# One quarter more of a dense layer's block in seven products: tiles 8 to 11 of block 1, and what moves with them

## The chip, the cores and the metric

The kernel runs on one core of a Trainium2 chip. The core has a matrix engine (TensorE, PE in the profile; its weight loads are the row PEld), a vector engine (DVE), an activation engine (ACT), a general engine (POOL) and a queue engine (SP), each with its own instruction stream; they meet through semaphores. Data moves between the chip's memory and the on-chip buffers by DMAs, which SP, ACT and POOL issue. The time is the device time of one execution in microseconds (us), and less is better. One time of the kernel before is the median of three runs; one further execution was profiled.

## The reference

The input x has 2048 rows of 1024 numbers. The rows are normalised, and the result is the sum of x, a state space branch A and a dense branch B:

```python
xn = _layernorm(x, axis=-1)
return x + _A_ref(xn, ...) + _B_ref(xn, B_w1, B_b1, B_w2)

# A: Lam_bar = exp(dt * Lam), complex
Bu = jnp.einsum("bld,pd->blp", x + 0j, B_bar)
for t in range(L):
    h = Lam_bar[None, :] * h + Bu[:, t, :]
y = 2.0 * jnp.einsum("blp,dp->bld", hseq, Cmat).real + x * Dskip[None, None, :]

# B: 1024 -> 3584 -> 1024
h = jnp.einsum("bsd,df->bsf", x, w1) + b1
sp = jnp.log1p(jnp.exp(-jnp.abs(h))) + jnp.where(h > 0, h, jnp.zeros_like(h))
act = h * jnp.tanh(sp)          # Mish
return jnp.einsum("bsf,fd->bsd", act, w2)
```

## The kernel before

The 2048 rows are worked in four blocks of 512 (`blk` 0 to 3). A block has these stages on PE: dense 1 (x by w1, 28 tiles of 128 columns), the input projection of branch A (x by B, complex), dense 2 (the activations by w2) and the output projection (the scanned state by C). DVE rotates the projected state, scans it over the 512 rows and rotates it back (`rotate_in`, `recur`); at the block's end it adds the two branches to x (`finish`, L1711).

**Plain tiles and quads.** In block 0 all of dense 1 is plain: for each tile, 8 matmuls of 128 x 512 (`first_tile`, L871). From block 1 on parts of it go in seven products: four tiles of w1 (a quad) and the block's 512 rows are split two by two, and seven products of halves stand for eight (`w_product`, L1024). One product is 8 matmuls of 128 x 256. Products 1, 2 and 4 take quarters of the scaled quad; 5, 6, 7 and 3 take sums and differences of quarters, and 5, 6, 7 and 4 sums of x (`sums_x`, L1840). A product lands in one of a quad's three PSUM banks (X, Y, Z; `F_BANKS`); 6, 7 and 4 add to what 1 left in X, and 3 to what 5 left in Z, so that `w_evacuate` must have read a bank before the next product adds to it. There are seven quads of w1, and in the order strings of the diff the letters p q s w x y z name them (`REAL` gives the place of each in w1): p is tiles 12 to 15, q 16 to 19, s 20 to 23, w 24 to 27, x, y and z are tiles 0 to 3, 4 to 7 and 8 to 11. The projection of branch A is done in the same way, for four pairs of column groups, a to d (`product`, L948; `evacuate`). In block 1 (`FAST`) before, tiles 0 to 11 are plain and p, q, s, w are quads; in blocks 2 and 3 (`SPLIT`) all seven are.

**A quad's way.** `w_load` (POOL, four DMAs) brings a quad to an on-chip place (`W_RAW`); `w_scale` (ACT, two instructions) scales it by a power of two; `w_keep` stores quarters 1, 2 and 4 to a scratch in memory (`wsd`); `w_sums` forms 5, 7, 6 and 3 in place (DVE, L1199) and stores them. PE reads quarters back through the ring, seven slots of 512 KB that SP fills in a fixed order of items (`ring_load`); an item's load waits until the slot's user seven items earlier is done. Quads in `ON_CHIP` read products 5, 6, 3 and 7 from the on-chip place.

**Order.** Nothing is scheduled at run time. The strings `WHOLE` (block 1), `STEPS` (block 2) and `LAST` (block 3) are written by hand and read from the left by `project_fast`: a letter and a number are one step (`a5`: product 5 of pair a; `z5`: product 5 of quad z), with its instructions on all engines. Others are `k0` (the next waiting sum on DVE), `P` (`sums_B`, L1833), `T` (`table_scale` on ACT), `V` (`w_scale` of quad s), `v` (of quad w), `h` (`d2_row`, a scaled row group of w2), `j` (`ln_skip`), `r` (`rotate_in`), `g` (Mish on a group of tiles), `u` (`open_unit`: six matmuls of dense 2 in one bank), `l` (the next block's x), `m`, `n` (loads), `Q` (`row_powers`), `S` (`row_scales`), `O` (a held DMA on SP). Each engine then works its own instructions strictly in this order. A DMA of ACT or SP stands in the same stream as its other instructions, and a wait holds up what follows.

**Around block 1.** At block 0's end DVE scales the B matrix and finishes the block (L1820, L1711); then, in `side(0)` of block 1, it forms sums for the projection (L1833), the sums of x (L1840), the sums of quads p and q (L1199) and scales the rest of B (L1820). ACT scales quads, issues block 0's four stores to the output (L1692) and then does the Mish of the plain tiles (L879). The sums of x are written where block 0's rows lay, so they wait for those stores. In block 1's scan, `w_exponent`, `row_powers` and `row_bound` work out scales that blocks 2 and 3 need.

## Time and profile before

| | us |
|---|---|
| median of three runs (lowest, highest) | 587.51 (587.39, 587.77) |
| the profiled execution's own time | 587.58 |
| its span, first to last instruction | 586.3 |
| PE busy in the span | 581.0 |
| DVE busy | 513.4 |
| ACT busy | 401.8 |
| POOL busy | 150.7 |

The span is 1.3 us shorter than the execution's own time; what lies around it is not in the trace. In a timeline a row gives the start (from the span's start), the length, the engine, the line, the operation with its tiles, the number of instructions merged in the row, and in brackets how long the engine had been idle before it and what ended that. Instructions of one engine overlap by up to 0.1 us, so several in a row take less than their number times one. A few per cent of the matmul records are missing, so a count in a row can be lower than the program's. Line numbers are those of the kernel before.

### The profile page before, as it was taken

Reading aid. Unit: us, or ns where it says so; the run is one execution under the profiler, and the core shown is the slowest. Engines: PE = TensorE matmul, PEld = TensorE weight load, DVE = VectorE, ACT = ScalarE, POOL = GpSimd, SP = SyncE. Lnnn points to the kernel's source line nnn. Section 1 sums busy time; section 2 is a strip of 40 time slices with the busy share of each in tenths; the row PEclk is TensorE's granted clock in tenths of the full one; section 3 lists DMA queues with packets and bytes.
Section 4 is the critical chain, followed back from the end, with each engine's and each line's share of the span. In section 5 each row is a group of like instructions: output and inputs, shape, how many; then the busy total and the mean of one; then the engine's idle time right before and its main releaser. Section 6 shows DMA issues by size and latency. Waiting matters only on the chain.

```text
span 586.3 us, 9768 instructions
## 1 busy us (share of the span) xinstructions
PE 581.0 (99%) x3599; PEld 353.9 (60%) x3635; DVE 513.4 (88%) x789; ACT 401.8 (69%) x541; POOL 150.7 (26%) x213
## 2 busy tenths in 40 slices
PE   9999999999999999999999999999999999999998
PEld 8644444444447887444448888644446888844444
DVE  6998999998997878999877889779999669789995
ACT  4859994658578868999916687959223798992330
POOL 2899300123524420441351241001010113100000
PEclk9999999999999999999999999999999999999999
DMA  9999998999688978999999899798865966998832
GB/s 244 306 243 247 245 186 202 316 301 360 185 303 287 357 249 293 316 321 255 345 375 345 305 309 382 257 344 209 306 210 191 346 237 241 326 324 318 293 113 73
DMA packets 116345, 162.15 MB, mean 277 GB/s; under 512 B 55882, under 2 KB 66762, under 8 KB 116298
## 3 DMA queue, kind: packets, MB, share of 16 engines
q1 hardware_dynamic: 99776, 109.67, 62.0%
q0 software_dynamic: 13440, 44.57, 21.7%
q10 hardware_dynamic: 3082, 7.29, 3.3%
q8 instruction: 29, 0.48, 0.3%
q14 instruction: 18, 0.15, 0.1%
HBM read 115.36 MB, written 34.08 MB: 255 GB/s over the span
## 4 chain that ended last, share of the span: by engine, by line
PE 93%; DVE 2%; ACT 2%; DMA 1%; issue 1%; POOL 0%; ACTq 0%; POOLq 0%
PE ps L1502 34%; PE ps L1024 19%; PE ps L948 13%; PE ps L1563 10%; PE ps L871 10%; PE ps L1438 5%; DMA act<-in_A_B_im_dram 1%; PE ps L680 1%; PE ps L689 1%; PE ps L642 1%; ACT act L894 1%; PE ps L1525 1%; ACT act L901 1%; DVE CT L835 0%; DVE CT L833 0%
## 5 line engine op out<-in xcount | busy, mean ns | idle before, releaser
L1502 PE MATMUL ps<-ring,act 128*128 128x512 bf16 x532 | 117.3, 379 | 0.6
L1502 PEld LDWEIGHTS ps<-ring,act 128*128 128x128 bf16 x544 | 53.2, 98 | 63.8
L1044 ACT ACTIVATE snaps<-ps,par,cs 128x256 f32<-128x256 f32 x100 | 54.4, 562 | 44.4 <-PE ps L1024 40.0
L1502 PE MATMUL ps<-ring,hT 128*128 128x512 bf16 x355 | 78.3, 379 | 0.4
L1024 PE MATMUL ps<-TT,ring 128*128 128x256 f16 x552 | 68.3, 273 | 0.0
L910 DVE TENSOR_TENSOR mt<-hT,tab 128x2048 bf16<-128x2048 bf16 (+1 forms) x56 | 67.9, 1213 | 0.4
L1502 PEld LDWEIGHTS ps<-ring,hT 128*128 128x128 bf16 x362 | 35.4, 98 | 42.7
L1453 DVE TENSOR_TENSOR_SCAN hT<-cs,qi,hT 128x512 bf16<-128x512 f32 x48 | 60.7, 1275 | 0.0
L1024 PEld LDWEIGHTS ps<-TT,ring 128*128 128x128 f16 (+1 forms) x552 | 53.8, 98 | 7.2 <-issue 0.2
L871 PE MATMUL ps<-xnT,ring 128*128 128x512 bf16 x258 | 56.8, 379 | 0.3
L1024 PE MATMUL ps<-xnT,ring 128*128 128x256 bf16 x424 | 53.9, 273 | 0.0
L1061 DVE SCALAR_TENSOR_TENSOR act<-ps,cs,snaps 128x512 bf16<-128x512 f32 x54 | 39.8, 748 | 15.2 <-PE ps L1024 13.3
L1024 PEld LDWEIGHTS ps<-xnT,ring 128*128 128x128 bf16 (+1 forms) x424 | 41.4, 98 | 5.4
L871 PEld LDWEIGHTS ps<-xnT,ring 128*128 128x128 bf16 x264 | 25.8, 98 | 30.9
L1230 POOL DMA_DIRECT2D w2d<-act x21 | 15.0, 718 | 110.5 <-ACT act L1240 54.9
L1473 ACT ACTIVATE hT<-hT,wz 128x1024 bf16<-128x1024 bf16 x16 | 18.1, 1146 | 34.3 <-DVE hT L1468 34.3
L1563 PE MATMUL ps<-ring,act 128*128 128x512 bf16 (+1 forms) x176 | 39.5, 379 | 0.2
L1230 POOL DMA_DIRECT2D w2d<-hb x28 | 20.0, 717 | 74.4 <-ACT hb L1240 33.0
L894 ACT ACTIVATE act<-act 128x2048 bf16<-128x2048 bf16 (+3 forms) x13 | 33.0, 2557 | 3.8 <-DVE act L1047 3.8
L973 DVE TENSOR_TENSOR hT<-ps,snaps 128x512 f16<-128x512 f32 x36 | 23.8, 687 | 12.3 <-ACT snaps L965 11.1
L1563 PEld LDWEIGHTS ps<-ring,act 128*128 128x128 bf16 (+1 forms) x180 | 17.6, 98 | 20.6
L1173 POOL DMA_DIRECT2D wsd<-hb x35 | 19.1, 548 | 39.0 <-DVE hb L1199 28.8
(240 smaller groups left out, 1085.2 us busy)
## 6 DMA issues: line engine op xcount, KB each, us to landing
ring<-wsd SPq DMA_DIRECT2D x122, 256.0 KB, 4.6
ring<-in_B_w_dram SPq DMA_DIRECT2D x54, 512.0 KB, 5.9
ring<-ctd SPq DMA_DIRECT2D x24, 512.0 KB, 4.4
ring<-w2d SPq DMA_DIRECT2D x24, 512.0 KB, 4.6
wsd<-hb POOLq DMA_DIRECT2D x35, 256.0 KB, 5.1
ring<-w2d SPq DMA_DIRECT2D x29, 256.0 KB, 3.8
w2d<-hb POOLq DMA_DIRECT2D x28, 256.0 KB, 5.5
w2d<-act POOLq DMA_DIRECT2D x21, 256.0 KB, 6.2
```

Source lines behind the costliest of these rows:

```text
L871: PE.mm(lambda e, k=k, w=w: e.matmul(ps[:, bank, :], lhsT=w, rhs=xnT[:, k, :], start=k == 0, stop=k == NK - 1), reads=[b_ring[s]] + b_xnT, ...
L894: aop(lambda e: e.activation(t, t, AF.Mish), reads=b, writes=b)
L910: vop(lambda e: e.tensor_tensor(mt[:], u.unsqueeze(1).to_broadcast([P, 2, 2, TB]), tab[:, :, j, :].unsqueeze(2).to_broadcast([P, 2, 2, TB] ...
L948: PE.mm(lambda e, w=w, x=x, o=o, begin=begin, end=end: e.matmul(ps[:, bank, o:o + TH], lhsT=w, rhs=x, start=opens and begin, stop=end, ski ...
L1024: PE.mm(lambda e, w=w, x=x, o=o, begin=begin, end=end: e.matmul(ps[:, bank, o:o + TH], lhsT=w, rhs=x, start=opens and begin, stop=end, ski ...
L1044: aop(lambda e, o=o, p=p, j=j: e.activation(o, p, AF.Identity, scale=ig, bias=b1(f0 + j)), reads=[b_ps[b], b_par, b_ig], writes=b_dst)
L1061: vop(lambda e: e.scalar_tensor_tensor(out=dst, in0=bank(b), scalar=ig, in1=src, op0=ALU.mult, op1=ALU.add), reads=[b_ps[b], b_snap[k], b_ ...
L1230: PO.dma(lambda e: e.dma_start(w2d[at // 4][:, at % 4 * TB:(at % 4 + 2) * TB].rearrange("p (j t) -> p j t", j=2), t[:, :, d, :]), sem, rea ...
L1438: PE.mm(lambda e, j=j, ci=ci, k=k, bank=bank: e.matmul(ps[:, bank + ci, :], lhsT=BT[:, ci, j, k, :], rhs=xnT[:, k, :], start=k == 0, stop= ...
L1453: vop(lambda e: e.tensor_tensor_scan(out=hT[:, ci, j, :], data0=cj("r", j).to_broadcast([P, TB]), data1=hT[:, ci, j, :], initial=init, op0 ...
L1502: PE.mm(lambda e: e.matmul(ps[:, u, :], lhsT=lhsT, rhs=rhs, start=st_, stop=last, skip_group_check=blk in SPLIT), reads=reads, writes=[b_p ...
L1563: PE.mm(lambda e: e.matmul(ps[:, bank, :], lhsT=lhsT, rhs=rhs, start=st_, stop=end, skip_group_check=True), reads=b_t + [b_ring[s]], write ...
```

## The change

Quad z (tiles 8 to 11) of block 1 leaves the plain tiles and becomes seven products. Its load and its scaling are done at block 0's end, its sums in block 1 behind those of quad q, and its sums' stores go on POOL; before, it was loaded and scaled in block 1's scan, its sums were formed at block 2's start, and SP stored them there. Products 5, 6, 3 and 7 of z read the on-chip place, which is now act 8 to 15. The order of block 1's products is written anew. `row_powers` for the late rows goes behind the last step of the scan, `row_bound` from the scan to block 2's start (step `S1`), and four sums for w2 go between the four `finish` steps of block 1 instead of ahead of them.

```diff
-    GROUPS = (... (20, 24), (24, 28))
-    TILES = [*range(12)]
+    GROUPS = (... (20, 24), (24, 28), (8, 12))
+    TILES = [*range(8)]
...
-    EARLY, LATE = ((0, 18), (26, 28)), ((18, 26),)
+    EARLY, LATE = ((0, NF),), ((18, 26),)
...
-    WHOLE = ("a2 a1 V0 b2 b1 a5 b5 V1 P4 P5 a6 b6 v6 P6 P7 a3 b3 P0 a7 b7 P1 Q0 n0 p1 q1 a4 b4 "
+    WHOLE = ("a2 a1 V0 b2 b1 a5 b5 V1 a6 b6 a3 b3 k0 k0 a7 b7 k0 k0 P4 P5 z1 q1 a4 b4 z5 P6 P7 v0 z2 q2 P0 P1 q5 z6 P2 q6 z3 P3 q3 T0 "
...
-    STEPS = ("p1 p5 p2 k0 k0 q1 k0 q5 p6 k0 q2 s1 k0 p7 ...
+    STEPS = ("p1 p5 p2 S1 q1 q5 p6 q2 s1 k0 p7 ...
...
-    F_BANKS = ((3, 1, 2), (7, 5, 6), (7, 5, 6), (3, 1, 2))
+    F_BANKS = {0: (3, 1, 2), 1: (7, 5, 6), 2: (7, 5, 6), 3: (1, 2, 3), 6: (3, 1, 2)}
...
-    ON_CHIP = [(5, n) for n in (5, 6, 3, 7)]
+    ON_CHIP = [(i, n) for i in (2, 5) for n in (5, 6, 3, 7)]
...
-    W_RAW = (("h", 0), ("h", 8), ("a", 0), ("h", 8), ("h", 0), ("a", 20), ("h", 8))
+    W_RAW = (("h", 0), ("h", 8), ("a", 8), ("h", 8), ("h", 0), ("a", 20), ("h", 8))
...
-                if i == 2:
-                    held.append(lambda queue: w_store(i, n, o, b_o, queue))
-                else:
-                    w_store(i, n, o, b_o)
+                w_store(i, n, o, b_o)
...
-                row_scales()
+                (row_scales, row_bound)[n]()
...
             elif kind == "v":
-                w_scale(n)
-                w_sums(n, True)
+                w_scale(6, (1 - n,))
+                if n:
+                    w_sums(6, True)
...
             finish(q, 0, len(units) * TB)
+            if blk == FAST:
+                later.pop(0)()
...
                     w_sums(3)
-                    w_load(6)
                     scale_B(2)
                     w_sums(4)
+                    w_load(6)
+                    w_sums(2, True)
                     scale_B(3)
-                if f in (1, 3, 4, 5):
-                    table_scale((1, 3, 4, 5).index(f))
...
                     next(out_stage)
-                    w_load(2)
                     for i in range(2):
                         w_abs(i)
-                    w_scale(2)
                     next(out_stage)
                 if j == 5:
                     w_exponent(1)
-                    row_powers(LATE)
-                    row_bound()
...
+                if j == NJ - 1:
+                    row_powers(LATE)
                     d2_scale(3)
...
         if blk == FAST:
-            for _ in range(4):
-                later.pop(0)()
-            for i in (2, 0, 1):
+            for i in range(2):
                 w_sums(i, True)
...
             w_load(4)
+            w_load(2)
...
             w_load(5)
             w_scale(3)
+            w_scale(2)
```

In block 0's last stage, on POOL: the loads of quads p and q into hb, four small products and the carry of the scan, then the load of quad s into act. Before:

```order
L1098 DMA hb<-in_B_w_dram 128x4x256 x8
L1995 TENSOR_TENSOR cs<-cs 128x8 x2
L1482 TENSOR_TENSOR qi<-hT,cs 128x8 x2
L1482 TENSOR_TENSOR qt<-hT,cs 128x8 x2
L1484 TENSOR_TENSOR qi<-qi,qt 128x8
L1486 TENSOR_TENSOR qi<-qi,qt 128x8
L1098 DMA act<-in_B_w_dram 128x4x256 x4
L1173 DMA wsd<-hb 128x1024 x10
```

and now:

```order
L1099 DMA hb<-in_B_w_dram 128x4x256 x8
L1099 DMA act<-in_B_w_dram 128x4x256 x4
L1994 TENSOR_TENSOR cs<-cs 128x8 x2
L1483 TENSOR_TENSOR qi<-hT,cs 128x8 x2
L1483 TENSOR_TENSOR qt<-hT,cs 128x8 x2
L1485 TENSOR_TENSOR qi<-qi,qt 128x8
L1487 TENSOR_TENSOR qi<-qi,qt 128x8
L1099 DMA act<-in_B_w_dram 128x4x256 x4
L1175 DMA wsd<-hb 128x1024 x3
L1175 DMA wsd<-act 128x1024 x3
L1175 DMA wsd<-hb 128x1024 x11
```

The load of z (four DMAs into act) stands ahead of the four products, and its three quarters' stores between those of p and q.

In block 1, on DVE: the last scaling of B (BT), the joins of the products of pairs a and b with what was kept of them (hT16_49 from PSUM and snaps), the sums of a quad (act) and the sums for the projection (SS_53, BT16_50). Before:

```order
L1820 TENSOR_TENSOR BT<-BT,act 128x2048 x2
L973 TENSOR_TENSOR hT16_49<-ps,snaps_54 128x2x256 x2
L1833 TENSOR_TENSOR SS_53<-BT 128x2x512
L1833 TENSOR_TENSOR SS_53<-SS_53,BT 128x2x512
L1833 TENSOR_TENSOR SS_53<-BT,SS_53 128x2x512
L1833 TENSOR_TENSOR BT16_50<-BT 128x2x512
L973 TENSOR_TENSOR hT16_49<-ps,snaps_54 128x2x256 x2
L1833 TENSOR_TENSOR SS_53<-BT 128x2x512
L973 TENSOR_TENSOR hT16_49<-ps,snaps_54 128x2x256 x2
```

and now:

```order
L1823 TENSOR_TENSOR BT<-BT,act 128x2048 x2
L974 TENSOR_TENSOR hT16_49<-ps,snaps_54 128x2x256 x4
L1201 TENSOR_TENSOR act<-act 128x1024 x2
L974 TENSOR_TENSOR hT16_49<-ps,snaps_54 128x2x256 x2
L1201 TENSOR_TENSOR act<-act 128x1024 x2
L1836 TENSOR_TENSOR SS_53<-BT 128x2x512
```

Two sums of quad z stand between the joins of products 1 and 3 and those of product 7 (the last two joins), and the sums for the projection stand behind them.

At the end of block 1's products, on PE: the last products of s and w (from the ring or from act) and the opening matmuls of dense 2 (L1502, now L1503). Before:

```order
L1024 MATMUL ps<-TT_52,act 128x256 x8
L1024 MATMUL ps<-TT_52,ring 128x256 x8
L1502 MATMUL ps<-ring,act 128x512 x6
L1024 MATMUL ps<-TT_52,ring 128x256 x16
L1502 MATMUL ps<-ring,act 128x512 x218
```

and now, from p4 and s4 on:

```order
L1025 MATMUL ps<-TT_52,ring 128x256 x16
L1025 MATMUL ps<-xnT,ring 128x256 x8
L1025 MATMUL ps<-TT_52,ring 128x256 x8
L1025 MATMUL ps<-xnT,ring 128x256 x8
L1025 MATMUL ps<-TT_52,ring 128x256 x8
L1503 MATMUL ps<-ring,act 128x512 x6
L1025 MATMUL ps<-xnT,ring 128x256 x8
L1503 MATMUL ps<-ring,act 128x512 x6
L1025 MATMUL ps<-TT_52,ring 128x256 x8
L1503 MATMUL ps<-ring,act 128x512 x6
L1025 MATMUL ps<-TT_52,ring 128x256 x8
L1503 MATMUL ps<-ring,act 128x512 x206
```

Three opening units instead of one stand among the last products of w, and the first of them comes four products behind s4.

More of the change, by code (lines that the diff above doesn't have):

```diff
@@ L338, in build_kernel @@
     (wp, b_wp), (wg, b_wg), (wq, b_wq) = wide("dt"), wide("xs"), wide("cr2")
+    b_wg = [b_wg, Buf("xs_late")]
     hsink = nc.alloc_sbuf_tensor_at("hsink", [P, D], bf16, offset=base_hb + 2 * 2 * GF * TB)
@@ L1070, in w_evacuate @@
         if n == 6:
-            keep["w", i, "v"] = snap(X, 0, VE if i == 6 else AC)
+            keep["w", i, "v"] = snap(X, 0, VE if i == 6 and blk != FAST else AC)
         if n == 3:
@@ L1130, in build_kernel @@
     mix = [(nc.alloc_sbuf_tensor_at("mx%d" % h, [P, 6 * SQ], f32, offset=at), b)
-           for h, (at, b) in enumerate(((base_hb, b_hbf[0]), (nc.lookup_mloc(act).addr + 17 * 2 * TB, b_actf[17])))]
+           for h, (at, b) in enumerate(((base_hb, b_hbf[0]), (nc.lookup_mloc(act).addr + 17 * 2 * TB, b_actf[17]),
+                                      (nc.lookup_mloc(mt).addr, b_m[0])))]
     def spread_down(t, b):
@@ L1240, in d2_row @@
         aop(lambda e: e.activation(o, x, AF.Copy, scale=wg[:, r:r + 1]),
-            reads=b_x + [b_wg], writes=b_t[2 * j:2 * j + 2])
+            reads=b_x + [b_wg[LATE[0][0] <= r < LATE[0][1]]], writes=b_t[2 * j:2 * j + 2])
         if n % 4 == 3:
@@ L1286, in row_powers @@
     def row_powers(parts):
+        b_g = b_wg[parts is LATE:]
         for lo, hi in parts:
```

20 lines of the change are left out of this document (10 added, 10 removed), and 6 rows, old and new, of the table WHOLE.

## The prediction

> **What bounds the kernel now.** I read the page's first two parts, then PE's waits, then the timeline of block 1 on each engine.
>
> ```profile
> PE 581.0 (99%) x3599; PEld 353.9 (60%) x3635; DVE 513.4 (88%) x789; ACT 401.8 (69%) x541; POOL 150.7 (26%) x213
> PEclk9999999999999999999999999999999999999999
> ```
>
> ```profile
> PE ps L642 <- DVE filler L468: 1.0, 1, 1.0
> PE ps L680 <- ACT xr L527: 0.2, 1, 0.2
> ```
>
> PE is busy in 99% of the span at the full granted clock, and its only listed waits lie in the first microseconds. Once under way PE waits for nobody. So matmul time that is removed shortens the end one for one, and every new wait of PE lengthens it one for one. The question is how many waits the new order brings.
>
> **The products.** PE's timeline at block 1's start:
>
> ```profile
> 161.04 20.88 PE L871 MATMUL ps<-xnT,ring 128*128 128x512 bf16 x94
> 181.76 3.66 PE L948 MATMUL ps<-xnT,BT 128*128 128x256 bf16 x32
> 185.25 3.66 PE L948 MATMUL ps<-TT,SS 128*128 128x256 f16 x32
> ...
> 217.61 1.04 PE L1024 MATMUL ps<-TT,act 128*128 128x256 f16 x8
> 218.48 1.91 PE L948 MATMUL ps<-TT,BT 128*128 128x256 f16 x16
> ```
>
> The program has 96 plain matmuls from 161.04 to 181.76 (two records are missing): 0.2158 us each. 32 of the half width take 181.76 to 185.25: 0.109 each, 0.873 a product of 8, and 217.61 to 218.48 is the same for weights read on-chip. Quad z costs 32 x 0.2158 = 6.91 before and 56 x 0.1091 = 6.11 after. **Term 1: -0.80.** That is 0.14% of the time and, with no other stall of PE to be removed, the ceiling of the gain. A bound for "no change" is 0.2%, or 1.17 us, about what a measurement of this kernel can tell.
>
> A rule speaks against this term. The Trainium skill, "TensorE: Matmul & The Clock Gate", section "Back-to-back issue gap", says that weight load and matmul together set the spacing, with about 131 ns a matmul at 512 columns and 81 ns at 128. By that 32 plain ones would cost 4.2 and 56 at least 4.5, so the term would be +0.3 at least. The rows above, 0.2158 and 0.109, disagree with it.
>
> **Earlier load and scaling.** The rows of POOL, then of ACT and DVE, at block 0's end:
>
> ```profile
> 148.18 2.97 POOL L1098 DMA_DIRECT2D hb<-in_B_w_dram  x4 [4.08 <-DVE CT L833]
> 155.33 0.36 POOL L1995 TENSOR_TENSOR cs<-cs 128x8 f32<-128x8 f32 x2 [4.18 <-DVE cs L1787]
> ```
>
> ```profile
> 160.77 4.07 ACTq L1692 DMA_DIRECT2D out_dram<-xx  x4
> 164.89 3.89 ACT L1184 ACTIVATE hb<-hb,cs 128x2048 bf16<-128x2048 bf16 x2 [10.43 <-DVE SS L1833]
> 168.80 1.28 ACT L879 ACT_TABLE_LOAD   x1
> 170.09 1.26 ACT L879 ACTIVATE act<-ps,par 128x512 bf16<-128x512 f32 x2
> ```
>
> ```profile
> 167.72 0.69 DVE L1840 TENSOR_TENSOR TT<-xnT,TT 128x1024 f16<-128x1024 bf16 x1 [0.21 <-DMA out_dram<-xx]
> 180.34 2.48 DVE L1820 TENSOR_TENSOR BT<-BT,act 128x2048 bf16<-128x2048 bf16 x2
> ```
>
> POOL's four DMAs of z take about 2.97 from 151.15 to 154.1, inside the 4.18 that POOL idles, so the carry behind them is not late. Landing is bounded by the neighbours in that queue:
>
> ```profile
> L1098 POOL DMA_DIRECT2D hb<-in_B_w_dram x4: 749/749/752, 148.2 to 150.4; - x4
> DMA to landing us min/median/max: 3.8/5.4/6.0
> ```
>
> The last of those lands by 150.4 + 6.0 = 156.4; four more at about 1 us each land by 160.4, bounded by 157.3 (3.8 after the first issue) and some 163. ACT's two scalings (3.89) then run from 160.4 to 164.3 in ACT's idle 10.43, ahead of the old 164.89. The output stores wait in the same stream behind the scalings' wait, first due at 160.77: by 160.4 they are free. Cost nothing, unless z lands after 160.8; then the stores slip, and with them DVE's sums of x, which already wait 0.21 for such a landing. z also adds 1 MB and three stores to the traffic there; I put 0 to 1.0 on that slip, and take 0.25, nearest to the 0.21.
>
> **DVE behind it: term 2.** From 167.72 DVE works without a pause to 180.34 + 2.48 = 182.82, and that stays, while PE starts its products 6.91 sooner, at 174.85. DVE's joins and sums:
>
> ```profile
> 205.38 2.86 DVE L1199 TENSOR_TENSOR hb<-hb 128x1024 f16<-128x1024 bf16 x4
> 216.35 2.48 DVE L973 TENSOR_TENSOR hT<-ps,snaps 128x512 f16<-128x512 f32 x4
> ```
>
> After 182.82 come four joins (2.48), two sums of z (half of 2.86) and the join of a7 (0.62): 187.3. PE's a4 adds to the bank that this join reads and is the fifteenth product: 174.85 + 14 x 0.873 = 187.07. So PE waits 0.25, some 0.05 for the signal, and the slip: 0.3 to 1.3, taken 0.3 + 0.25. **Term 2: +0.55.** Later joins have room: z7's ends at about 198.5 for z4 at 199.3. s4 comes one product after s7, whose join (0.7 and its signal) leaves nothing: +0.05 (0 to 0.3), **term 3**.
>
> ACT loses four Mish of single tiles and gains 8 instructions of evacuation and one Mish of four tiles; DVE gains three joins and saves five small operations. At block 1's start ACT is earlier than PE needs: eight Mish from 170.09 at 0.58 free the first banks by 173.6, before 174.85.
>
> **The opening units: term 4.** u4 reads three w2 items. The third goes into the slot that p4 and s4 free, so its load is issued after s4. Until u4's fifth matmul lie four products and four matmuls, 3.49 + 0.86 = 4.35, less some 0.2 for the issue: the load has 4.1. Before, this slot was freed 8 us ahead of u4. Loads of that kind, in this stretch and overall:
>
> ```profile
> L458 SPq DMA_DIRECT2D ring<-in_B_w_dram x5: 367/368/368, 221.3 to 232.2; - x5
> DMA to landing us min/median/max: 3.8/4.6/6.2
> ...
> ring<-in_B_w_dram SPq DMA_DIRECT2D x54, 512.0 KB, 5.9
> ```
>
> So PE waits 0 (3.8) to 2.1 (6.2); I take 4.5, near the stretch's median because the load of w2 rows (m0) is over by then: **+0.40**. The Trainium skill, "DMA: Bandwidth & Descriptors", section "Anatomy of one DMA", gives 2.0 us and bytes over 436 GB/s, 3.2 us for 512 KB. By that estimate term 4 is 0 and the sum 0.4 lower; the shortest landing above, 3.8, is already longer.
>
> **Ring, SP and the sums' stores.** Two loads of 512 KB leave the ring and three of 256 KB enter. q5 and q6 are read some 8 us sooner, at 191.4, but their stores no longer stand behind a load on POOL: formed by 179.7, stored and loaded back by about 188. z5's store must land before z2's join writes its place at 192.2; it is issued at 186.1. Room in both, no cost; if z5 landed 2 us late, z4 would wait some 0.5. In block 2 four SP stores and four sums (2.86) go, and `row_bound` (2.7) comes: nothing.
>
> **The end of block 1.** Mish and row scalings now alternate on ACT, and DVE's four w2 sums wait for their stores to land before the scan starts.
>
> ```profile
> 227.55 2.18 ACT L1240 ACTIVATE hb<-hb,cs 128x1024 bf16<-128x1024 bf16 x2
> 234.49 7.30 ACT L894 ACTIVATE act<-act 128x2048 bf16<-128x2048 bf16 x4
> ```
>
> ```profile
> 244.64 3.63 DVE L1453 TENSOR_TENSOR_SCAN hT<-cs,qi,hT 128x512 bf16<-128x512 f32 x3
> 253.62 0.18 DVE L596 RECIPROCAL ln<-ln 128x4 f32<-128x4 f32 x1 [1.19 <-ACT ln L594]
> 279.38 0.17 DVE L1290 TENSOR_SCALAR cs<-cs 128x8 f32<-128x8 f32 x1 [1.53 <-ACT CT L1283]
> 280.15 0.20 DVE L1301 SCALAR_TENSOR_TENSOR cs<-par 128x28 f32<-128x28 f32 x1
> 282.69 0.15 DVE L1309 COPY wz<-mx 128x1 f32<-128x1 f32 x1
> 296.88 2.93 DVE L1261 TENSOR_TENSOR act<-act 128x1024 f16<-128x1024 bf16 x4
> 301.70 1.23 DVE L1711 TENSOR_TENSOR xx<-ps,xx 128x1024 bf16<-128x1024 f32 x1 [1.89 <-PE ps L1502]
> 308.02 1.12 DVE L1047 TENSOR_SCALAR snaps<-ps,cs,par 128x256 f32<-128x256 f32 x2
> ```
>
> With w4 done near 234.8, one evacuation (1.1), four Mish (7.3) and four row scalings (4.3) end at about 247.7; a store of 0.7 and a landing of some 5 follow, then two sums: the scan starts near 254.5, ten later. DVE gets back the three waits (1.19 + 1.53 + 1.89), `row_bound` (2.7) and the sums (2.93) that leave the stretch: 10.2. So the first `finish` is just in time; one more sum behind the last `finish` moves p1's snap end from 309.14 to 309.9, and block 2's p6, which adds to that bank, is due at 306.68 + 5 x 0.873 = 311.05. Cost 0, with 1.1 of room.
>
> **Sum.** -0.80 + 0.55 + 0.05 + 0.40 = +0.2 against the profiled execution's 587.58, so 587.8; the median of the runs is 0.07 below it: **587.7**.
>
> **Rivals.**
> - *The gain arrives whole:* DVE is early at a7 and the w2 load lands in 4.1. For it: the shortest landings; against: DVE's unbroken row of work. 587.51 - 0.80 = 586.7.
> - *z lands late* (slower): if its last part lands at 163 instead of 160.4, stores, sums of x and all of DVE slip 2.2. a4 then waits 2.5; with terms 1, 3 and 4 that is +2.15, 589.7. It decides from a landing of about 162 on. Against it: ACT's and POOL's idle rows.
> - *u4's load takes 6.2:* term 4 is 2.1 and the sum +1.9, 589.4; it decides from 5.5.
> - *The scan comes too late:* stores landing 3 us later use up the 1.1 and hold block 2's p6 for 1.9: +2.1, 589.6.
> - *Half-width products cost more than their row* (the rule on spacing, here 56 at 81 ns against 32 at 131): +0.3 instead of -0.80, 588.8. The rows leave it little.
>
> **Numbers.** Forecast with some of terms 2 to 4: 0.38. Whole gain: 0.16, also within 0.2%. z late 0.14, u4's load 0.11, scan 0.12, dearer products 0.02, other new waits of over 2 us 0.04: all slower. Faster by over 0.2%: 0.03, since the ceiling lies below it. So faster 0.03, same 0.54, slower 0.43. The range goes from the whole gain, 586.6, to the sum of two of the slower cases' excesses, 590.6; the likeliest case's own is 586.9 to 588.6.
>
> **What would show it.** Term 1: 64 plain matmuls, then z's products at 0.873. Term 2: PE idle ahead of a4 (L948), ended by DVE's L973. Term 4: PE idle within u4 (L1502), ended by a ring load. Scaling: the output stores still at 160.8. End: DVE's first `finish` still waiting for PE. The forecast is wrong if PE idles elsewhere by more than 1 us, above all at block 2's start.

## The result and the profile after

The changed kernel takes 594.25 us (median of 6 runs, 592.41 to 596.04), the kernel before beside it 587.74 (6 runs, 587.39 to 588.02). The ratio is 1.0107, with a 95% interval of 1.0087 to 1.0128: slower by 1.1%. The forecast was 587.7 with a range up to 590.6, so it was wrong. Two things are new: PE waits at seven places, and the runs scatter over 3.6 us where those of the kernel before scatter over 0.6.

The profiled execution took 592.74 us, 5.16 more than the profiled one of before. PE's waits in it are these (engine, line, what it waited for: us in total, times, longest):

```profile
PE ps L1503 <- DMA ring<-in_B_w_dram: 1.4, 2, 0.7
PE ps L949 <- ACT snaps L966: 1.0, 1, 1.0
PE ps L1025 <- ACT snaps L1045: 0.7, 1, 0.7
PE ps L1025 <- DVE snaps L1048: 0.7, 1, 0.7
PE ps L1025 <- DVE act L1062: 0.3, 1, 0.3
```

What they cost is read better from the starts in PE's timeline, since the ends of matmuls overlap the next start:

```profile
161.23 13.98 PE L872 MATMUL ps<-xnT,ring 128*128 128x512 bf16 x64
...
182.03 1.91 PE L949 MATMUL ps<-xnT,SS 128*128 128x256 bf16 x16
184.94 1.92 PE L949 MATMUL ps<-TT,BT 128*128 128x256 f16 x16 [1.00 <-ACT snaps L966]
...
196.30 1.04 PE L1025 MATMUL ps<-xnT,ring 128*128 128x256 bf16 x8
197.47 1.05 PE L1025 MATMUL ps<-TT,act 128*128 128x256 f16 x8
198.52 1.05 PE L1025 MATMUL ps<-TT,ring 128*128 128x256 f16 x8
199.40 1.91 PE L949 MATMUL ps<-xnT,BT 128*128 128x256 bf16 x16
201.59 1.91 PE L1025 MATMUL ps<-TT,ring 128*128 128x256 f16 x16 [0.28 <-DVE act L1062]
...
229.68 0.59 PE L1503 MATMUL ps<-ring,act 128*128 128x512 bf16 x2
230.96 0.60 PE L1503 MATMUL ps<-ring,act 128*128 128x512 bf16 x2 [0.69 <-DMA ring<-in_B_w_dram]
232.29 0.61 PE L1503 MATMUL ps<-ring,act 128*128 128x512 bf16 x2 [0.73 <-DMA ring<-in_B_w_dram]
232.74 1.04 PE L1025 MATMUL ps<-xnT,ring 128*128 128x256 bf16 x8
...
313.53 1.04 PE L1025 MATMUL ps<-TT,ring 128*128 128x256 f16 x8
315.28 1.05 PE L1025 MATMUL ps<-TT,ring 128*128 128x256 f16 x8 [0.71 <-DVE snaps L1048]
...
322.33 1.04 PE L1025 MATMUL ps<-TT,ring 128*128 128x256 f16 x8
324.08 1.03 PE L1025 MATMUL ps<-TT,ring 128*128 128x256 f16 x8 [0.71 <-ACT snaps L1045]
```

With 0.873 a product and 1.295 for six matmuls of 512 columns:

| place | working | PE loses |
|---|---|---|
| a7 | 184.94 - (182.03 + 1.75) | 1.16 |
| z7, q7, z4 | 197.47 - 197.17, 198.52 - 198.34, 201.59 - 201.15 | 0.92 |
| u4 | 232.74 - 229.68 - 1.295 | 1.76 |
| block 2: p6 and q7 | 315.28 - 314.40, 324.08 - 323.20 | 1.76 |
| sum | | 5.60 |

The first block of plain matmuls is 64 long instead of 96, and z's products stand at 0.873 each, so the -0.80 is there. 5.60 - 0.80 is 4.80 of the 5.16; the rest is a start of block 1 that is 0.19 later (161.23 for 161.04) and some waits of 0.1.

The wait ahead of **a7**, on DVE and ACT:

```profile
181.10 2.48 DVE L1823 TENSOR_TENSOR BT<-BT,act 128x2048 bf16<-128x2048 bf16 x2
183.50 1.28 DVE L974 TENSOR_TENSOR hT<-ps,snaps 128x512 f16<-128x512 f32 x2
...
184.30 1.18 ACT L966 COPY snaps<-ps 128x512 f32<-128x512 f32 x2 [1.32 <-DVE hT L974]
```

DVE's row of work ends at 183.58. Its first joins give back the buffers of what ACT keeps of a product; ACT, idle for 1.32, copies a6 only then, and a7 adds to the bank that this copy reads.

The waits near **z7 and z4**: z2's join writes act 8 and 9, where sum 5 of z lies, so the store of that sum has to land first. It left at 187.28 and took 8.0:

```profile
187.28 0.55 POOL L1175 DMA_DIRECT2D wsd<-act  x1 [0.65 <-DVE act L1201]
```

```profile
DMA to landing us min/median/max: 8.0/8.0/8.0
```

```profile
195.40 1.41 DVE L1062 SCALAR_TENSOR_TENSOR act<-ps,cs,snaps 128x512 bf16<-128x512 f32 x2 [2.51 <-ACT snaps L1045]
```

187.28 + 8.0 is 195.28; the join starts 0.12 later (the engine named in the bracket had long been done). ACT's copy of z6 needs the buffer that this join returns, and z7 needs that copy.

At **u4** the three w2 loads, issued from 220.2 to 226.4, took up to 9.4:

```profile
L459 SPq DMA_DIRECT2D ring<-in_B_w_dram x3: 368/383/383, 220.2 to 226.4; - x3
...
DMA to landing us min/median/max: 5.8/8.1/9.4
```

Before **block 2** the scan starts at 259.06 instead of 244.64:

```profile
256.20 2.94 DVE L1260 TENSOR_TENSOR hb<-hb 128x1024 f16<-128x1024 bf16 x4 [9.33 <-DMA w2d<-hb]
259.06 3.63 DVE L1454 TENSOR_TENSOR_SCAN hT<-cs,qi,hT 128x512 bf16<-128x512 f32 x3
...
305.42 1.22 DVE L1712 TENSOR_TENSOR xx<-ps,xx 128x1024 bf16<-128x1024 f32 x1
308.29 0.69 DVE L1260 TENSOR_TENSOR act<-act 128x1024 f16<-128x1024 bf16 x1 [1.65 <-DMA w2d<-act]
...
314.10 1.12 DVE L1048 TENSOR_SCALAR snaps<-ps,cs,par 128x256 f32<-128x256 f32 x2
```

DVE is idle for 9.33 until the stores of w2's scaled rows have landed. It gives 10.7 of the 14.4 back (259.06 to 305.42 is 46.4; before, 244.64 to 301.70 was 57.1), but waits once more, 1.65, for the landing of a store, and copies p1's bank until 315.22, where p6 was due at 314.40.

### The profile page after: what moved, and what is told of

It is laid out like the page before. It is cut to its first block, busy times and chain, and to the rows that moved or that the text cites. A ratio compares the mean times of both kernels' runs of the same rounds, so it can differ in the third digit from the quotient of the medians.

```text
span 591.5 us, 9858 instructions
## 1 busy us (share of the span) xinstructions
PE 583.7 (99%) x3659; PEld 355.3 (60%) x3659; DVE 511.6 (86%) x787; ACT 406.2 (69%) x546; POOL 152.5 (26%) x217
## 4 chain that ended last, share of the span: by engine, by line
PE 78%; DVE 9%; ACT 5%; DMA 5%; issue 3%; POOL 0%; DVEq 0%; ACTq 0%; SPq 0%
PE ps L1503 25%; PE ps L1025 16%; PE ps L1564 11%; PE ps L949 11%; PE ps L872 6%; PE ps L1439 5%; DVE hT L1454 3%; DMA w2d<-act 2%; ACT hb L1186 1%; DVE mt L911 1%; PE ps L681 1%; PE ps L690 1%; DMA out_dram<-xx 1%; DMA ring<-in_B_w_dram 1%; ACT act L895 1%
## 5 line engine op out<-in xcount | busy, mean ns | idle before, releaser
L1503 PE MATMUL ps<-ring,act 128*128 128x512 bf16 x544 | 118.7, 379 | 1.4 <-DMA ring<-in_B_w_dram 1.4
L1503 PEld LDWEIGHTS ps<-ring,act 128*128 128x128 bf16 x544 | 53.0, 98 | 65.3 <-DMA ring<-in_B_w_dram 2.4
L1045 ACT ACTIVATE snaps<-ps,par,cs 128x256 f32<-128x256 f32 x106 | 57.6, 562 | 42.5 <-PE ps L1025 34.6
L1503 PE MATMUL ps<-ring,hT 128*128 128x512 bf16 x362 | 78.6, 379 | 0.0
L1025 PE MATMUL ps<-TT,ring 128*128 128x256 f16 x560 | 70.5, 273 | 1.7 <-ACT snaps L1045 0.7
L1503 PEld LDWEIGHTS ps<-ring,hT 128*128 128x128 bf16 x362 | 35.4, 98 | 42.7
L1062 DVE SCALAR_TENSOR_TENSOR act<-ps,cs,snaps 128x512 bf16<-128x512 f32 x57 | 41.9, 748 | 21.8 <-PE ps L1025 16.3
L1025 PEld LDWEIGHTS ps<-TT,ring 128*128 128x128 f16 (+1 forms) x560 | 54.3, 98 | 10.2 <-issue 1.5
L1025 PE MATMUL ps<-xnT,ring 128*128 128x256 bf16 x440 | 55.7, 273 | 0.0
L872 PE MATMUL ps<-xnT,ring 128*128 128x512 bf16 x232 | 50.4, 379 | 0.0
L1025 PEld LDWEIGHTS ps<-xnT,ring 128*128 128x128 bf16 (+1 forms) x440 | 42.9, 98 | 5.9 <-issue 0.3
L872 PEld LDWEIGHTS ps<-xnT,ring 128*128 128x128 bf16 x232 | 22.7, 98 | 27.2
L895 ACT ACTIVATE act<-act 128x2048 bf16<-128x2048 bf16 (+3 forms) x14 | 35.0, 2511 | 3.8 <-DVE act L1048 3.8
```

The costliest lines, as they stand in the source:

```text
L872: PE.mm(lambda e, k=k, w=w: e.matmul(ps[:, bank, :], lhsT=w, rhs=xnT[:, k, :], start=k == 0, stop=k == NK - 1), reads=[b_ring[s]] + b_xnT, ...
L895: aop(lambda e: e.activation(t, t, AF.Mish), reads=b, writes=b)
L1025: PE.mm(lambda e, w=w, x=x, o=o, begin=begin, end=end: e.matmul(ps[:, bank, o:o + TH], lhsT=w, rhs=x, start=opens and begin, stop=end, ski ...
L1045: aop(lambda e, o=o, p=p, j=j: e.activation(o, p, AF.Identity, scale=ig, bias=b1(f0 + j)), reads=[b_ps[b], b_par, b_ig], writes=b_dst)
L1062: vop(lambda e: e.scalar_tensor_tensor(out=dst, in0=bank(b), scalar=ig, in1=src, op0=ALU.mult, op1=ALU.add), reads=[b_ps[b], b_snap[k], b_ ...
L1503: PE.mm(lambda e: e.matmul(ps[:, u, :], lhsT=lhsT, rhs=rhs, start=st_, stop=last, skip_group_check=blk in SPLIT), reads=reads, writes=[b_p ...
```

## The experiments

The time of the changed kernel scatters by more than most single causes cost, so the first runs are read by PE's waits, and those in which one cause is put back into a version without waits by the time as well. The kernel before, run beside each of them, took 587.7 to 587.8 every time (medians). Waits of PE without a row are worked out from the starts as in the table. Below each diff stands what was expected before the run; the diffs are cut, "..." marks what is left out.

**1. rows_early.** The row scalings (h) ahead of the last product and the Mish:

```diff
-r3 u6 T7 w4 l0 u7 g8 g4 h0 r4 g5 h1 r5 h2 g6 r6 h3 g7 r7 k0 k0 k0 k0
+r3 u6 T7 h0 h1 h2 h3 w4 l0 u7 g8 g4 r4 g5 r5 g6 r6 g7 r7 k0 k0 k0 k0
```

> The changed kernel with one move: the four row scalings of w2 (h0 to h3) stand ahead of the last product w4 and of the five Mish, in the 3.99 us that ACT idled there, instead of between the Mish. Theory: block 2's two waits of PE (0.88 each) come from the scan's late start, since DVE sat idle for 9.33 us ahead of it, until the stores of these rows had landed. It expects that idle time to be under 2 us, the scan to start at about 250 instead of 259.06, both waits in block 2 gone, and the time 1.8 shorter than the changed kernel's. Rival (the scales of the late rows, now set behind the scan, hold up group 3's scaling on ACT): the two waits stay or shrink by less than half. Third (PE is held there by the extra sums between the four finishing steps): the first of the two waits stays at 0.7 or more.

591.30 (9 runs, ratio 1.0043 to 1.0081), 3.0 less than the changed kernel. DVE has no idle time ahead of the sums, the scan starts at 251.45 instead of 259.06, and PE has no wait in block 2:

```profile
251.45 3.63 DVE L1454 TENSOR_TENSOR_SCAN hT<-cs,qi,hT 128x512 bf16<-128x512 f32 x3
```

As the theory had it, with more gain in the time (1.8 was expected) than these two waits explain.

**2. late_in_scan and late_again.** The late rows' scales where they were before:

```diff
                     w_exponent(1)
+                    row_powers(LATE)
...
-                    row_powers(LATE)
                     d2_scale(3)
```

> The changed kernel with the late rows' scales set where they were before, inside the scan behind the exponents of w1, and their bound still at block 2's start. Theory (the late start of the scan costs block 2's two waits): ACT works without a pause from 290.50 to 306.51 and needs the late rows' scales only for its last eight row scalings, from 298.09, while DVE had set them by 296.54, so nothing is won: both waits stay at 0.7 to 1.0, the time is within 0.5 of the changed kernel's. Rival (the place behind the scan is the cause): both waits gone, 1.7 shorter.

> The changed kernel with the late rows' scales back inside the scan, once more with more rounds: the first time block 2's two waits stayed (1.26 and 0.92) but the median of its 4 runs, 592.55, was 1.7 under the changed kernel's. Theory (the place of these scales does not matter): the two waits stay, 1.5 to 2.5 in sum, and the median goes to 593.5 to 595, as the changed kernel's 594.25 and 594.48. Rival (something in it is worth 1.7, though not through these waits): the median stays at 592 to 593.

592.55 (4 runs) and 593.21 (6 runs). The two waits in block 2 stayed, 1.26 and 0.92 in the first profile, 1.56 and 0.82 in the second, so these scales are not their cause. The time lies 1.0 to 1.9 under the changed kernel's in both, inside its scatter but in the same direction twice; the second median lies between the limits of its theory and its rival. What the two profiles have less of is the wait at a7 (0.46 and 0.12), which lies ahead of everything that was moved; whether there is a gain of another kind stays open.

**3. scale3_later.** DVE's last scaling of B behind z's sums (a new step `f3`):

```diff
-a3 b3 k0 k0 a7 b7 k0 k0 P4 P5
+a3 b3 k0 k0 a7 b7 k0 k0 f3 P4 P5
...
                     w_sums(2, True)
-                    scale_B(3)
```

> The changed kernel with DVE's last scaling of B (two instructions, 2.48 us) moved from in front of the first joins to behind the second pair of z's sums. Theory: PE's wait of 1.16 ahead of a7 is DVE's backlog, which delays the first joins to 183.50, so that ACT gets no free buffer for what it keeps of a6 until 184.30. It expects the first join at about 181.1, the wait ahead of a7 gone, z5's sum and its store some 2 us sooner, and with that a part of the three small waits (0.29, 0.17, 0.44) near z7 and z4 gone too: 1.2 to 2.0 shorter than the changed kernel. Rival (ACT's own scaling of quad s, 2.0 us at 180.97, holds the evacuation of a6): the wait ahead of a7 stays above 0.8.

594.39 (4 runs): no gain. The wait ahead of a7 was gone, as expected, but PE then waited near z7:

```profile
194.93 1.04 PE L1025 MATMUL ps<-xnT,ring 128*128 128x256 bf16 x8
197.13 1.05 PE L1025 MATMUL ps<-TT,act 128*128 128x256 f16 x8 [1.17 <-ACT snaps L1045]
```

z2's join started at 195.07, hardly sooner than 195.40. PE came 1.4 sooner (195.80 for 197.17) and waited 1.33 for the same landing: the first wait had hidden most of the second. The cause of the wait was right, its worth was not. That is not the whole of it: in this profile PE also waits longer in block 2, 1.55 and 1.53 instead of twice 0.88, and why is not shown.

**4. load0_later.** The load of quad x for block 2 behind w4:

```diff
-c7 d7 j2 n0 p1 s1
+c7 d7 j2 p1 s1
...
-w4 l0 u7
+w4 l0 n0 u7
```

> The changed kernel with the load of quad x for block 2 (four DMAs, 1 MB, issued from 214.50 to 216.74) moved behind the last product w4. Theory A (traffic): the three w2 loads for u4 took 9.4, 8.1 and 5.8 us because this load and two of w2's rows run beside them; without it they land 1.5 to 3 us sooner and u4's two waits (0.85 and 0.89) fall to 0.6 or less in sum, 1.2 to 1.7 shorter than the changed kernel. Theory B (the slot is freed too late, whatever the traffic): the third load is issued at 226.43 as before, takes 5 or more, and the two waits stay at 1.2 or more in sum.

```profile
DMA to landing us min/median/max: 5.2/6.1/7.4
```

The loads of u4, the same three, land some 2 sooner than 5.8, 8.1 and 9.4, and PE's waits there fall from 1.76 in sum to one of 1.14, for the third load. Neither limit was met: the traffic had set the first two landings, and for the third, issued when its slot came free, 5.2 was still too long. 593.99 (4 runs), within the scatter.

**5. u4_after_w3.** u4 one product later:

```diff
-r2 u4 w3 u5 T5 w7 T6 r3 u6
+r2 w3 u4 T5 w7 u5 T6 r3 u6
```

> The changed kernel with the opening units one product later: w3 ahead of u4, and u5 behind w7. Theory (the loads land at a time that the slots and the traffic set, whatever PE does): u4's due time is 0.87 later, so its waits fall from 1.74 in sum to 0.7 to 1.0 and no new wait comes at w7 or w4: 0.8 shorter. Rival (a later user also delays the loads behind it): the sum of waits at the units and at the first matmuls of dense 2 stays at 1.5 or more.

```profile
DMA to landing us min/median/max: 6.9/8.1/9.4
```

u4 lost 1.83, all at the third load, which took 6.9 here and 5.8 in the changed kernel: the later due time was used up. By its limit that is the rival, but its reason (PE delays the loads' issue) holds for 0.5 only, 226.93 for 226.43; the rest is a longer landing. 593.49 (4 runs). With this move and the last together, in version 13 below, u4 doesn't wait.

**6. load6_back.** The load of quad w ahead of q's stores:

```diff
                     w_sums(3)
+                    w_load(6)
                     scale_B(2)
                     w_sums(4)
-                    w_load(6)
```

> The changed kernel with one move on POOL: the load of quad w (four DMAs, 1 MB) stands ahead of the stores of q's sums, where it was before, instead of behind them. Theory: the waits near z7 and z4 come from the landing of the store of z's sum 5, which z2's join has to wait for (issued 187.28, landed 195.28, join at 195.40); it is in a queue with the 1 MB issued from 182.01. Issued from about 179, in a stretch with a DMA share of 0.60, that load is over sooner: z5's store lands by 193.5, the waits of 0.29, 0.17 and 0.44 go, the wait ahead of a7 stays (0.5 to 2.2 in the runs so far): 0.5 to 1.0 shorter. Rival (the ring's loads alone fill the transfers from 184 on): z5's store lands after 194.8 and the waits stay.

z2's join starts at 192.64 without a wait, and the three small waits are gone, as expected; a7's stayed (1.24). So it was the 1 MB issued ahead of z5's store:

```profile
192.64 1.41 DVE L1062 SCALAR_TENSOR_TENSOR act<-ps,cs,snaps 128x512 bf16<-128x512 f32 x2
```

593.33 (4 runs).

**7. load6_scale3.** Both moves, 3 and 6 together:

> Both moves: DVE's last scaling of B behind z's sums, and the load of quad w ahead of the stores of q's sums. With the scaling alone moved the wait ahead of a7 was gone, but PE then waited 1.33 near z6, at the same landing of z5's store. Theory (two waits in a row, the second behind the first): with both moves both are gone, and from 175 to 203 PE loses less than 0.6, against 2.1 in the changed kernel. Rival (the landing of z5's store doesn't depend on the load): PE still loses 1.2 to 2 there.

From 175 to 203 PE lost 0.44, as the theory had it (0.36 of it for q5's ring load, since q's stores now stand behind the load). The time doesn't show it: 593.88 (4 runs), within the scatter. The profiled execution took 590.54, the lowest of the four; the others 592.11 to 597.12.

**8. all_five.** Moves 1, 3, 4, 5 and 6 together:

> The changed kernel with all five moves: row scalings ahead of the Mish, the last scaling of B behind z's sums, the load of quad w ahead of q's stores, the load of quad x behind w4, u4 behind w3. If the waits found are the whole of the loss, PE's waits between 160 and 330 fall from 5.9 to under 1.5 in sum, and the time goes to 587.0 to 588.6, beside 587.8 for the kernel before: no measurable difference, since the products save 0.80. If every removed wait only uncovers another landing behind it, the time stays above 590.

592.68 (7 runs, 590.72 to 599.12): above 590, as when a removed wait uncovers another, but only one of the two new waits is a landing. The named waits were gone; 1.76 had come for q5's ring load, the price of move 6, and 1.57 for w4's evacuation on ACT, behind the four row scalings of move 1.

**9. load6_later.** The load of quad w the other way, behind z's stores, and its two scalings later:

```diff
-a7 b7 k0 k0 P4 P5 z1 q1 a4 b4 z5 P6 P7 v0 z2 q2 ... z3 P3 q3 T0 z7 v1 q7 T1
+a7 b7 k0 k0 n6 P4 P5 z1 q1 a4 b4 z5 P6 P7 z2 q2 ... z3 P3 q3 T0 v0 z7 q7 T1 v1
...
                     w_sums(4)
-                    w_load(6)
                     w_sums(2, True)
```

> The changed kernel with the load of quad w moved the other way, behind the stores of z's sums (issue from about 191 instead of 182), and its two scalings on ACT each some 6 us later, to follow it. Ahead of q's stores (the earlier try) it freed z2's join but pushed q's stores and so the ring's load of q5. Theory: behind z's stores it holds up nobody: z5's store lands by 193.5, the waits near z7 and z4 (0.90 in sum) go, q5 doesn't wait; the wait ahead of a7 stays. 0.5 to 1.0 shorter than the changed kernel. Rival: the traffic of 182 to 206 (over 400 GB/s) only moves, and PE waits as long for a ring load between 191 and 206 or for w1 at 225.

598.24 (4 runs): the rival, and more than it asked. The load landed at 205.95, ACT stood in front of its scaling, and the copy of a projection behind it held PE for 5.3 (the wait at a7 was 2.9 in this profile):

```profile
205.97 2.00 ACT L1186 ACTIVATE hb<-hb,cs 128x2048 bf16<-128x2048 bf16 x1 [5.45 <-DMA hb<-in_B_w_dram]
```

**10. five_other.** Moves 3, 4, 5 and 9, and the row scalings in another form (the diff is against all_five):

```diff
-w3 u4 T5 w7 u5 T6 r3 u6 T7 h0 h1 h2 h3 w4 l0 n0 u7 g8
+w3 u4 T5 h0 w7 u5 h1 r3 u6 h2 h3 w4 l0 n0 u7 T6 T7 g8
```

> Five moves again, two of them in another form: the load of quad w behind z's stores, and the row scalings of w2 each behind one of the last products, with two scalings of rotation tables (T6, T7) put behind w4, so that w4's evacuation isn't held up as in the first version (1.57). With it DVE's last scaling of B behind z's sums, the load of quad x behind w4, u4 behind w3. If these waits are the whole of the loss, PE's waits from 160 to 330 are under 1.2 in sum, the profiled time is 587.0 to 588.5 and the median under 589. If the traffic only hands the wait on to the next transfer, the sum of waits stays over 2.5.

594.27 (4 runs); by their sum, 4.6, the waits are on the rival's side. But all of them were gone save one of 0.44 and the one of move 9, here 4.2, after which PE ran at half its rate for 5. Without the 4.2 and what followed it the profiled time would be some 587.6 (an estimate: 594.26 less 4.2 less half of 5), so that the place of one load seemed all that was left to find.

**11. before_rows_late.** The kernel before with only the row scalings moved:

```diff
-r1 w2 w6 h1 s3 w3 s7 h2 w7 r2 u4 s4 w4 r3 h3 u5 l0 u6 u7 g4 r4 g5 r5 g6 r6 k0 k0 g7 r7 k0 k0
+r1 w2 w6 s3 w3 s7 w7 r2 u4 s4 w4 r3 u5 l0 u6 u7 g4 h0 r4 g5 h1 r5 h2 g6 r6 h3 g7 r7 k0 k0 k0 k0
```

(h0, too, is taken from behind s6.)

> The kernel before with the one move alone: the four row scalings of w2 between the last Mish, as in the change, and the four sums behind the last rotation. Theory: this alone costs time, without quad z: the scan starts 6 to 11 later than 244.64 (its end reaches the finishing steps late), DVE has 4.6 of waits to give back before block 2, so PE waits 1 to 3.5 in block 2's first products: 588.8 to 591.0. Rival (the late scan hurts only together with the extra sums and the late rows' scales of the change): no wait of PE over 0.5 in block 2, within 0.5 of 587.8.

589.66 (10 runs, ratio 1.0018 to 1.0043): 1.9 slower by this move alone, in the middle of what was expected. In the profiled execution, the slowest of the ten (592.80), the scan starts at 252.97, and block 2's first product waits for a finishing step:

```profile
310.26 1.07 PE L1024 MATMUL ps<-xnT,ring 128*128 128x256 bf16 x8 [2.77 <-DVE xx L1711]
```

**12. changed_again.** The changed kernel once more:

> The changed kernel once more, as a control beside the others of this call and for a second profile. The waits at a7, near z7 and z4, at u4 and at block 2's p6 and at its p4 or s2 come back at the same places, each to within 1 us; the median lies between 592.4 and 596.

594.48 (4 runs, 591.85 to 595.47; profile 593.61). The waits stand at the same places: 1.15 at a7 (it was 1.16), 1.93 near z7 and z4 (0.92), 1.32 at u4 (1.76), 1.19 and 0.71 in block 2 (0.88 each; the second product is q7, behind p4).

**13. z_sums_first.** As 10, but z's sums 5 and 7 ahead of the joins and the load of quad w right behind their stores (the diff is against 10):

```diff
-a5 b5 V1 a6 b6 a3 b3 k0 k0 a7 b7 k0 k0 n6 f3 P4 P5
+a5 b5 k0 k0 n6 V1 a6 b6 a3 b3 a7 b7 k0 k0 f3 P4 P5
```

> As the last version with five moves, but z's sums 5 and 7 stand on DVE ahead of the joins of a6 to a7's products, and the load of quad w behind their stores, some 5 sooner than in that version, ahead of z's other two sums. There the only large wait left (4.2, and PE at half its rate for 5 after it) was a projection's evacuation on ACT behind the scaling of quad w, whose load landed at 201.66. Theory: issued from about 184, the load lands by 197, the scaling of w starts at 197 to 199 and holds up nothing, z5's store lands by 192: PE's waits from 160 to 330 are under 1.2 in sum, the profiled time is 586.8 to 588.3, the median under 589. If the traffic from 182 to 206 is the limit itself, some transfer is again waited for and the sum of waits is over 2.5.

588.25 (10 runs, 587.50 to 589.28), ratio to the kernel before 0.9997 to 1.0017, as expected in the median and in the waits (the profiled 588.35 lies 0.05 above its range): 6.0 of the 6.5 us are back, and the scatter is down from 3.6 to 1.8. PE's only wait beyond those of block 0's beginning is

```profile
PE ps L1025 <- DMA ring<-wsd: 0.7, 1, 0.7
```

at q3, 0.90 by the starts. With seven products in it, z neither costs nor saves time that can be measured.

**14 to 16. One cause put back into 13.** zf_rows_back: the row scalings between the Mish. zf_scale3_back: `scale_B(3)` in front of the joins. zf_u4_back: u4 ahead of w3 and n0 ahead of m0. The diff is that of the first:

```diff
-T5 h0 w7 u5 h1 r3 u6 h2 h3 w4 l0 n0 u7 T6 T7 g8 g4 r4 g5 r5 g6 r6 g7 r7
+T5 w7 u5 r3 u6 w4 l0 n0 u7 T6 T7 g8 g4 h0 r4 g5 h1 r5 h2 g6 r6 h3 g7 r7
```

> The version with z's sums first and five moves (588.25 beside 587.68 for the kernel before), with one cause put back: the four row scalings of w2 between the Mish, as in the change. Theory: the scan starts some 6 to 9 later than without, DVE's finishing steps and w2's sums come late to block 2, and PE waits 1.2 to 3 there in sum: 589.5 to 591.5. Rival (the late scan costs only in company with the other waits): no wait over 0.5 in block 2, within 0.4 of 588.25.

> The same version with DVE's last scaling of B put back in front of the first joins. Theory: DVE's backlog of 2.48 delays the joins that free ACT's buffers: PE waits 1 to 2.5 ahead of a7, and z's sums and the load of quad w behind them are 2.5 later, so ACT's scaling of w may hold another evacuation: 589.2 to 592. Rival (ACT's own row of work sets a7): no wait ahead of a7, within 0.4 of 588.25.

> The same version with u4 ahead of w3 again and the load of quad x back in front of w2's rows. Theory: u4 waits for its w2 loads, 1.2 to 2.2 in sum: 589.3 to 590.6. Rival (the loads were late only since the traffic behind the other waits was late): under 0.5 there.

| put back | median (runs) | against 588.25 | PE's waits in its profile | at p7 |
|---|---|---|---|---|
| row scalings | 592.32 (4) | +4.1 | block 2: 2.21 and 0.91; within the output projection 1.43 | 0.61 |
| scaling of B | 590.64 (6) | +2.4 | a7: 0.85; a projection's product due at 205.85: 0.44 | 0.86 |
| u4 and n0 | 590.30 (6) | +2.1 | u4: 0.74 and 1.02 | 0.61 |

The times of the second and third lie in their ranges; that of the first is 0.8 above its own, with 3.1 of waits in block 2 where at most 3 were expected; the second's wait at a7, 0.85, is under the 1 that was the least expected. The waits of the first in block 2 come where they came in the changed kernel:

```profile
314.77 1.05 PE L1025 MATMUL ps<-TT,ring 128*128 128x256 f16 x8 [2.05 <-DVE snaps L1048]
```

The wait at p7 belongs to none of the three: run 17, measured beside them with nothing put back, has it too (0.79), and 13's profile has not. So run 17's 588.53 is the fairer measure: against it the three cost 3.8, 2.1 and 1.8, and the 95% intervals of their ratios (from 1.0062, 1.0039 and 1.0031 up) all lie above run 17's (up to 1.0029). Their sum is 7.7, without the place of w's load, while the changed kernel is only 5.7 above 588.53: the waits partly stand behind one another.

**17. zf_c2_split.** The last wait of 13:

```diff
-q6 z3 P3 q3 T0 ... Q0 c2 d2 z4
+q6 z3 P3 c2 q3 T0 ... Q0 d2 z4
```

> The same version with one product moved: c2 ahead of q3 instead of behind q7, since the one large wait left (0.90) is that of q3 for its ring load, which landed at 196.21. Theory: q3's due time is 0.87 later, the wait falls under 0.2, and no other comes (z4 stands two products behind z7 instead of three, at most 0.4): 587.3 to 588.1, within 0.2% of the kernel before, since the products' saving of 0.80 is nearly used up by waits of 0.1 to 0.2 each. Rival (the ring's later loads move with PE): the wait stays above 0.6.

588.53 (10 runs, ratio 1.0007 to 1.0029), above the 588.1 expected. q3 no longer waits, but in this profile a7 does (0.63 by the starts) and p7, due at 220.95 (0.79), places that were free in 13:

```profile
PE ps L1025 <- ACT snaps L1045: 0.6, 1, 0.6
PE ps L949 <- ACT snaps L966: 0.5, 1, 0.5
```

No gain: what is left over changes from one profile to the next.

## Why the prediction was wrong

**Term 1, -0.80: right.** The products cost what the rows of before said, and PE was the bound.

**Earlier load and scaling: right, the slip too small.** z was scaled at 158.95 and 160.86 and the output stores left from 160.10 to 163.51. But the sums of x waited 1.02, 0.18 and 0.34 for these stores instead of 0.21, and DVE's row of work ended at 183.58 instead of 182.82: a slip of 0.76 where 0.25 was taken and up to 1.0 allowed.

**Term 2, +0.55: the wrong path, at the wrong product.** The cause was right (DVE is late: runs 3 and 15). The step followed only the bank from DVE to PE, and so came to a4, the fifteenth product. It left out ACT's four buffers: a6's copy waits for a buffer that DVE's first join returns, which stops PE at a7, the eleventh. It measured 1.16 and 1.15 in the two profiles of the changed kernel, but 0.12 to 2.18 in the five versions that leave everything up to a7 as it is (runs 1, 2, 4 and 5). That most of these lie inside the term's own range of 0.3 to 1.3 is luck, since a4 itself didn't wait.

**Term 3, +0.05:** s4 lost some 0.15.

**Term 4, +0.40: mis-sized, by the choice of row.** It took 4.5 for a load, near the median of five loads issued between 221.3 and 232.2 in the trace of before. The first two of these took 5.9 and 6.2, and the third load of the changed kernel, issued at 226.43, took 5.8. And the step held the third load alone for late: the first two took 9.4 and 8.1, like the loads just ahead of those five (9.0 and 9.9), and PE waited at the second too. In sum 1.76, near the rival with a load of 6.2 (2.1), which decided from 5.5 and had a chance of 0.11. The estimate that the prediction sets beside this term is stated in the Trainium skill, "DMA: Bandwidth & Descriptors", section "Anatomy of one DMA", for DMAs that GpSimd issues; these loads are issued by SP, and the measured times decide.

**Ring, SP and the sums' stores, "room in both, no cost": wrong.** It saw the place (z5's store ahead of z2's join) and gave it to 192.2. The store took 8.0 and the join started at 195.40. What it missed is what goes with it: the load of quad w, moved behind q's stores, stands shortly ahead of z5's store on POOL (three stores of quad s lie between) in the stretch in which the ring fills. That cost PE 0.92; run 6 moves this load alone, and the join no longer waits. The windows of the changed kernel end with the DMA share and GB/s; the kernel before has 351 and 337 GB/s in them:

```profile
190.00:198.00 8.00, 7.87 (x73) 6.83 (x71) 5.35 (x9) 6.70 (x11) 1.41 (x3) 1.00 1.04 408
198.00:206.00 8.00, 7.72 (x70) 6.45 (x69) 7.76 (x17) 7.57 (x10) 3.23 (x6) 1.00 1.05 405
```

**The end of block 1, "cost 0, with 1.1 of room": wrong, the largest error.** The scan was forecast at 254.5 and came at 259.06: PE had finished w4 at 237.9, three later than the 234.8 of the forecast, since the waits at a7, z7, z4 and u4 lay ahead of it, so the rows were scaled by 250.67 instead of 247.7; and all four sums stood ahead of the scan, not two (2.94 from 256.20 on). The 10.2 that DVE would give back were 10.7, so that part was right; the landing of the next store (1.65) was not in the sum at all. So p1's copy ended at 315.22, 5.3 later than the 309.9 of the forecast; the room of 1.1 and PE's own delay (p6 was due at 314.40 instead of 311.05) took 4.5 of it, and PE waited for the rest. The place is that of the rival "the scan comes too late" (2.1, chance 0.12), with 1.76, but its condition, stores that land 3 later than forecast after their issue, did not come: the stores were issued late and landed after 4.4 at most. That the move costs time by itself is shown: 1.9 in the kernel before, 3.8 beside run 17.

**The other rivals.** z was scaled in time, so it didn't land late, and half-width matmuls stand at 0.109 at the full granted clock after the change too, so they are no dearer than their row. The whole gain is there in the products, but in none of these runs in the time.

**The range and the chances.** The cases were added two at a time at most, and the sum is off: the excesses of u4's load (1.7) and of the scan (1.9) over the forecast would end the range at 591.3, not at 590.6; the runs began at 592.41. Nor were the cases independent: each is a place where a buffer, a slot or a landing had been early enough by less than a product or two, and a wait at one shifts PE against the transfers at the next. Four of them came together, which no sum of two holds.

## What to carry to other kernels

Where PE is busy for 99% of the span, the gain of a cheaper product has a ceiling that one row gives, while each of the kernel's slacks (a buffer's return, a slot, a landing, a store ahead of an overwrite) is a possible loss of the same size: list them all, price each by transfers of the same stretch, and add them rather than choose among them. Follow a late engine through every resource that it returns, not only through the data. If a wait is removed and the time stays, look for the wait behind it, and judge causes by putting them back, one by one, into a version without waits.

## What the hardware showed

After some longer waits PE runs at half its rate for about 3.4 us. In the profile of rows_early PE waited 2.0 at a7 (2.2 by the starts); the windows there have a granted clock (the column behind POOL) of 1.00 in the 0.6 us after it, then 0.50 for 3.4, then 1.00:

```profile
186.00:186.60 0.60, 0.60 (x7) 0.54 (x6) 0.60 (x2) 0.37 (x1) 0.60 (x2) 1.00 1.07 294
186.60:190.00 3.40, 3.40 (x18) 2.41 (x16) 3.37 (x6) 0.00 (x0) 2.04 (x4) 0.50 0.94 275
190.00:194.00 4.00, 4.00 (x38) 3.60 (x37) 3.65 (x6) 3.32 (x7) 1.08 (x2) 1.00 1.03 383
```

3.4 at half the rate is another 1.7 lost. The same stands behind the waits of 2.8 in before_rows_late and 5.1 in load6_later; with the wait of 4.0 in five_other it lasts for twice 3.4, from 207.6, within the wait, to 214.4. It does not stand behind a wait of 2.8 in load6_later at 184.4 nor behind those of 1.7 to 2.1 elsewhere. The Trainium skill, "TensorE: Matmul & The Clock Gate", section "Part 1: The HAM clock gate", describes a clock that halves after an idle window of some 3.4 us, with windows that run freely. The 3.4 agrees with the length of the stretches. The idle time does not: here waits of 2.0 and 2.8 were enough, and the measurement decides. Windows that run freely might explain why one wait halves the clock and a longer one does not; no run here shows where a window begins.

So a wait of 2 or more can cost more than its length. How often that happens can be read from each run's mean granted clock. One stretch of 3.4 at half the rate takes 0.3% off the mean over 590 us, and the runs show 1.0, 0.997 or 0.994, as none, one or two stretches would. All runs of the kernel before beside these, and all of version 13, show 1.0. Of the changed kernel's first six, only the one of 596.04 shows 0.997; the other five, 592.41 to 594.53, still scatter over 2.1, and load0_later's 596.96 shows 1.0. So the half rate is one reason for the scatter of these kernels and not the whole; the waits themselves differ from run to run, as a7's does.
